# The first two blocks' gate and value products in halves of 128 tokens, taken from whichever job is ready

## The chip, the cores and the metric

The kernel runs on one core of a Trainium2 chip. The core has a matrix engine (TensorE, PE in the profile; its weight loads are the row PEld), a vector engine (VectorE, DVE), a scalar engine (ScalarE, ACT), GpSimd (POOL) and SyncE (SP), which here only issues transfers. Each engine works through its own queue of instructions. The metric is the device time of one execution in microseconds, as the median of several runs.

## The reference

Top-k attention feeds a SwiGLU feed-forward block. Everything is float32.

```python
# attention: batch 8, heads 8, sequence 576, head_dim 64, top_k 32
scores = scale * np.matmul(q, k.transpose(0, 1, 3, 2))
kth = np.partition(scores, -top_k, axis=-1)[..., -top_k:-top_k + 1]
scores = np.where(scores >= kth, scores, -1000000000.0)
scores = scores - np.max(scores, axis=-1, keepdims=True)
attn = np.exp(scores)
attn = attn / (np.sum(attn, axis=-1, keepdims=True) + 1e-09)
x = np.matmul(attn, v)            # then (B,H,S,D) -> (B*S, H*D) = 4608 x 512
# feed-forward: d_model 512, d_ff 1536
g = x @ w_gate
silu = g * (1.0 / (1.0 + np.exp(-g)))
out = (silu * (x @ w_val)) @ w_out
```

## The kernel before

**Units.** Attention is cut into 160 units (batch, query tile, head pair), the head pair running fastest. A batch has four full query tiles of 128 rows and a fifth of 64 rows, in which a unit does half the work (both heads stand side by side). So units 0–15 are full, 16–19 half, 20–35 full again. One turn of the main loop (lines 750 to 810) writes out instructions for several units at different stages. In loop n:

- On even n, PE computes the scores of units n+1 and n+2 (line 306, tile `s`, copied by ACT at line 311 to `sc`), and the products with v of units n-4 and n-3 (line 424, tile `av`), which ACT copies to `xT` (line 440). `xT[kb]` is the transposed input of a feed-forward block of 256 tokens, and `done[kb]` counts what has been written of it.
- ACT weighs unit n-1 (lines 353 and 358: a threshold, then Exp with its sum in `tot`). Its bias comes from a small POOL subtraction (line 341).
- DVE selects the top 32 of unit n by four rounds of MAX8 (line 326) with MATCH_REPLACE8 (line 330) between them. Near the end of the unit comes `normalize` of unit n-1: two DVE instructions on `tot` (lines 369 and 370), and then a multiplication of `e` on POOL (line 376) or ACT (line 374).
- PE transposes the weights of unit n-2 (`turn`, line 390, tile `etps`), and ACT copies them (line 391).

**Rounding of the weights.** The three weight matrices pass through a rounding step in 36 pieces: 24 of gate and value, interleaved by columns, and then 12 of the output matrix. Each piece is a load (line 104, on SP's queue, into one of three `w` buffers), three ACT instructions (112, 114, 115), one on DVE (119) and two on POOL (120, 121). The generator `weights` is advanced by DVE's steps through units 0 to 14, and `ready[0]` tells how many pieces have been written out. A load waits until line 121 has read the buffer that it takes.

**Feed-forward.** There are 18 blocks of 256 tokens. `feed(kb)` is a generator. For each of six steps s it computes the gate product and the value product of two 128-wide slices of d_ff (line 480: 4 contraction chunks, moving operand 256 tokens wide). Every float32 product is two passes in the profile, so counts there are doubled. For the gate, ACT does Tanh, a halving and an addition (505 to 507) and POOL a multiplication (508). For the value it is an ACT copy (512) and a POOL multiplication (513). Block 0 then multiplies by the output matrix directly (line 526, tile `o_ps`); later blocks use seven quarter products instead (line 566, tiles `y_ps` and `x_ps`), with sums and differences on POOL. These need combinations of the output weights, which are built on POOL (lines 169 to 185), most of them only after block 0 no longer needs the plain ones (`plain_done`).

**What sets the order.** No scheduler changes it: every engine executes in the order in which the main loop writes. `pieces(k)` takes up to k feed-forward pieces, as long as `credit` is at least 1. A piece is one slice of gate or value (cost 1), two slices of the output product (cost 1) or half a quarter product (cost 0.75). `share(n)` gives the credit of a loop: a budget, 7.0 before the combined weights exist and 6.4 after, less what PE does for attention in that loop. In a loop `pieces` is called ahead of `turn` for up to two pieces and behind it for the rest. `piece()` (line 670) starts a block only when the whole of its `xT` has been written (`done[kb]` equal to 4 x 256); otherwise it returns 0 and the credit stays unspent. ACT's and POOL's share of a product is put on the lists `on_act` and `on_pool`, and written out at the next flush.

So before the change, block 0 can't begin until query tiles 0 and 1 have been through `av`, in loop 10.

Of the kernel before, what the change touches and what calls it, by code (L numbers as in the profile page):

```python
# [8 lines left out]
AF = mybir.ActivationFunctionType  # L9
ALU = mybir.AluOpType  # L10
FP32 = mybir.dt.float32
# [4 lines left out]
P = 128  # L16
# [4 lines left out]
BLK = 256  # L21
# [4 lines left out]
def kernel(  # L26
# [37 lines left out]
    nc = tc.nc  # L64
# [138 lines left out]
    def need(n):  # L203

        while ready[0] < n:
            next(weight)

    pairs = [(b, hp) for b in range(B) for hp in range(NHP)]
    raw, preps = {}, {}
# [252 lines left out]
    def flush(queue):  # L462
        while queue:
            queue.pop(0)()

    def feed(kb):


# [19 lines left out]
                    on_act.append(lambda: then(ps))  # L488
                yield 1

        plain = kb == 0
        first, late = slice(0, P), slice(P, BLK)

        s32 = x[:].rearrange("p a b -> p (a b)")[:, 0 : MQ * P].rearrange(
            "p (m t) -> p m t", t=P
        )

        for s in range(MS):
            h = ffn.tile([P, 2, BLK], FP32, tag="h", name="h", bufs=MS + 1)
            hs.append(h)  # L500


            def gate(ps, h=h):
                half = ffn.tile([P, 2, BLK], FP32, tag="gv", name="half_g", bufs=3)
                nc.scalar.activation(h[:], ps[:], AF.Tanh, scale=0.5)
                nc.scalar.mul(half[:], ps[:], 0.5)
                nc.scalar.add(h[:], h[:], 1.0)  # L507
                on_pool.append(lambda: nc.gpsimd.tensor_mul(h[:], h[:], half[:]))  # L508

            def value(ps, h=h, s=s):  # L510
                val = ffn.tile([P, 2, BLK], FP32, tag="gv", name="val", bufs=3)
                nc.scalar.copy(val[:], ps[:])  # L512
                on_pool.append(lambda: nc.gpsimd.tensor_mul(h[:], h[:], val[:]))  # L513

            yield from product(wg, s, gate)
            yield from product(wv, s, value)
        o = ffn.tile([P, 2, DM], FP32, tag="o", name="o", bufs=1)
        if plain:
            for t in range(2):
                ps = ps_f.tile([P, DM], FP32, tag="f", name="o_ps")  # L520
                for m in range(MC):
                    need(4 * MS + m + 1)
                    if m == 6:
                        flush(on_act)
                        flush(on_pool)
                    nc.tensor.matmul(  # L526
                        ps[:],
                        hs[m // 2][:, m % 2, t * P : (t + 1) * P],
                        wo[:, m, :],
                        start=(m == 0),  # L530
                        stop=(m == MC - 1),
                    )
                    if m == MC - 1:

                        def finish(ps=ps, t=t):
                            nc.scalar.copy(o[:, t, :], ps[:])
                            store(o[:, t, :], kb * BLK + t * P)

                        on_act.append(finish)
                        if t == 1:  # L540
                            plain_done.append(True)
                    if m % 2 == 1:
                        yield 1
            return
        while len(T[3]) < MQ:
            next(weight)
        DH = DM // 2
# [5 lines left out]

        def quarter(i, ps):
            for m in range(MQ):
                s, r = m // 2, m % 2
                lhsT = {
                    1: lambda: hs[s][:, r, first],
                    2: lambda: hs[s + MS // 2][:, r, first],
                    3: lambda: hs[s][:, r, late],  # L560
                    4: lambda: hs[s + MS // 2][:, r, late],
                    5: lambda: hs[s][:, r, late],
                    6: lambda: s32[:, m],
                    7: lambda: s32[:, m],
                }[i]()
                nc.tensor.matmul(  # L566
                    ps, lhsT, T[i][m], start=m == 0, stop=m == MQ - 1
                )
                if m % 3 == 2:
                    yield 0.75  # L570

        for s in range(MS // 2):
            nc.gpsimd.tensor_tensor(
                s32[:, 2 * s : 2 * s + 2], hs[s][:, :, first], hs[s][:, :, late], ALU.subtract
            )
        yield from quarter(1, y_ps[:, 0])
        flush(on_act)
# [1 line left out]

        for s in range(MS // 2):  # L580
            nc.gpsimd.tensor_tensor(
                hs[s][:, :, late], hs[s][:, :, late], hs[s + MS // 2][:, :, late], ALU.add
            )
        yield from quarter(7, x_ps[:, 1])
        for s in range(MS // 2):
            nc.gpsimd.tensor_tensor(
                s32[:, 2 * s : 2 * s + 2], hs[s][:, :, late], hs[s][:, :, first], ALU.subtract
            )
        yield from quarter(5, x_ps[:, 0])
        a = ffn.tile([P, 2, DH], FP32, tag="gv", name="p57", bufs=3)  # L590
# [21 lines left out]
        flush(on_pool)  # L612
        for s in range(MS // 2):
            nc.gpsimd.tensor_tensor(
                hs[s][:, :, late],
                hs[s + MS // 2][:, :, first],
                s32[:, 2 * s : 2 * s + 2],
                ALU.subtract,
            )
# [44 lines left out]
        on_act.append(rest_x)  # L664

    NU = len(units)
    todo = list(range(NBLK))
    current = []

    def piece():  # L670

# [1 line left out]
            flush(on_act)  # L673
        if len(on_pool) > 1:
            flush(on_pool)
        while True:
            if not current:
                if not todo or done.get(todo[0], 0) < NHP * BLK:
# [182 lines left out]
```

## Time and profile before

| what | us |
|---|---|
| median of 3 runs | 1770.41 (1769.8 to 1771.77) |
| the profiled execution, its own time | 1768.76 |
| its span in the profile | 1767.0 |
| PE busy | 1674.1 (95%) |
| DVE busy | 1483.2 (84%) |
| ACT busy | 1258.6 (71%) |
| POOL busy | 797.3 (45%) |
| chain that ended last, PE's share | 83% |

Busy time is a share of the whole span and hides that the stages differ. In the first 125 us PE is busy for about half of the time and DVE for nearly all of it; from there to the end of attention, near 1700 us, PE is busy for almost all of the time; the last 60 us are the feed-forward work of the last block. The column PEclk in the stretches is the clock granted to PE, as a share of full speed. In the lines of a timeline the first number is the start in us from the start of the span, the second the duration of the group, and the brackets at the end hold the idle time of that engine just before, with what ended it.

### The profile page before, as it was taken

The page shows a single profiled execution, that of the slowest core. Times are in us where ns is not written, and L with a number is a line of the kernel's source. Part 1 is how long each engine was busy: PE and PEld are TensorE (multiplying, and loading weights), DVE is VectorE, ACT ScalarE, POOL GpSimd, SP SyncE. Part 2 cuts the span into 40 slices and gives each one's busy share as a digit, 9 for nine tenths or more (in the row PEclk, how much of TensorE's full clock was granted, in tenths as well). Part 3 has the DMA queues.
Part 4 walks back from the last instruction along what each step waited for, and adds up shares of the span by engine and source line. Part 5 has one row for each costly group of instructions (what it writes and reads, how often), then busy time and mean ns, then how long its engine had stood idle before and what let it go on. Part 6 is the DMA issues. An engine that isn't in the chain of part 4 may idle for free.

```text
span 1767.0 us, 31028 instructions
## 1 busy us (share of the span) xinstructions
PE 1674.1 (95%) x11012; PEld 1386.1 (78%) x11012; DVE 1483.2 (84%) x3371; ACT 1258.6 (71%) x2869; POOL 797.3 (45%) x910
## 2 busy tenths in 40 slices
PE   4559999799999999999999999999999999999999
PEld 3338678687888878888888878888888878888887
DVE  6999898998899899998998988898989889988300
ACT  7789777777767686768777786777776776676531
POOL 4778444334353525353435424444335433535334
PEclk7669999899999999999999999999999999999999
DMA  7443030002100030001200030000300020000000
GB/s 195 130 119 87 27 80 1 13 1 68 30 5 9 14 79 6 13 1 43 54 13 1 13 71 27 1 13 8 90 1 13 1 54 17 13 1 13 1 13 12
DMA packets 109307, 59.68 MB, mean 34 GB/s; under 512 B 88544, under 2 KB 96992, under 8 KB 109152
## 3 DMA queue, kind: packets, MB, share of 16 engines
q1 hardware_dynamic: 108016, 57.37, 12.4%
q8 instruction: 87, 1.43, 0.3%
q14 instruction: 68, 0.56, 0.1%
q10 hardware_dynamic: 1136, 0.33, 0.1%
HBM read 48.23 MB, written 9.44 MB: 33 GB/s over the span
## 4 chain that ended last, share of the span: by engine, by line
PE 83%; DVE 6%; ACT 6%; POOL 3%; issue 1%; SPq 1%; DMA 1%; ACTq 0%; POOLq 0%
PE f L480 40%; PE av L424 9%; PE x_ps L566 9%; PE s L306 7%; PE etps L390 7%; PE y_ps L566 6%; DVE m L326 3%; DVE e L330 2%; PE s L292 2%; ACT e L358 2%; PE kqps L261 1%; PE o_ps L526 1%; ACT e L353 1%; POOL wo L121 1%; ACT et L391 1%
## 5 line engine op out<-in xcount | busy, mean ns | idle before, releaser
L326 DVE MAX8 m<-e 128x8 f32<-128x576 f32 x864 | 615.6, 749 | 3.3
L330 DVE MATCH_REPLACE8 e<-m,e 128x576 f32<-128x576 f32 x576 | 424.1, 743 | 0.0
L480 PE MATMUL f<-xT,wg 128*128 128x256 f32 x1728 | 400.9, 381 | 0.0
L480 PE MATMUL f<-xT,wv 128*128 128x256 f32 x1728 | 399.6, 380 | 0.0
L480 PEld LDWEIGHTS f<-xT,wg 128*128 128x128 f32 x1728 | 323.0, 190 | 50.7 <-issue 8.8
L480 PEld LDWEIGHTS f<-xT,wv 128*128 128x128 f32 x1728 | 323.0, 190 | 49.1 <-issue 7.9
L508 POOL TENSOR_TENSOR h<-h,half_g 128x512 f32<-128x512 f32 x108 | 137.8, 1276 | 353.5 <-ACT h L507 353.3
L358 ACT ACTIVATE e<-e,bias 128x576 f32<-128x576 f32 x288 | 221.1, 775 | 30.5 <-POOL bias L341 27.7
L513 POOL TENSOR_TENSOR h<-h,val 128x512 f32<-128x512 f32 x108 | 137.7, 1275 | 196.0 <-ACT val L512 177.8
L390 PE MATMUL etps<-ident,e 128*128 128x128 f32 (+1 forms) x1312 | 183.4, 282 | 44.1 <-ACT sc L311 20.7
L390 PEld LDWEIGHTS etps<-ident,e 128*128 128x128 f32 (+1 forms) x1312 | 155.3, 143 | 75.4 <-POOL e L376 21.3
L330 DVE MATCH_REPLACE8 e<-m,sc 128x576 f32<-128x576 f32 x288 | 212.0, 743 | 0.0
L353 ACT ACTIVATE e<-sc,m 128x576 f32<-128x576 f32 x288 | 211.1, 785 | 1.3 <-DVE m L326 1.3
L326 DVE MAX8 m<-sc 128x8 f32<-128x576 f32 x288 | 203.4, 743 | 9.1 <-ACT sc L311 9.1
L311 ACT ACTIVATE sc<-s 128x288 f32<-128x288 f32 x512 | 167.1, 413 | 58.8 <-PE s L306 58.5
L306 PE MATMUL s<-kqT 64*128 64x288 f32 x1024 | 175.2, 454 | 34.7 <-ACT et L391 19.3
L391 ACT COPY et<-etps 128x512 f32<-128x512 f32 (+1 forms) x448 | 183.1, 488 | 24.5 <-PE etps L390 24.0
L376 POOL TENSOR_TENSOR e<-e,tot 128x576 f32<-128x576 f32 x140 | 160.2, 1148 | 85.4 <-DVE tot L370 79.1
L369 DVE TENSOR_SCALAR tot<-tot 128x1 f32<-128x1 f32 x288 | 36.0, 145 | 189.6 <-ACT e L358 189.5
L306 PEld LDWEIGHTS s<-kqT 64*128 64x128 f32 x1024 | 96.5, 195 | 82.8 <-issue 25.7
L424 PE MATMUL av<-et,v 128*64 128x128 f32 (+1 forms) x2560 | 161.1, 270 | 0.0
L374 ACT ACTIVATE e<-e,tot 128x576 f32<-128x576 f32 x148 | 118.2, 799 | 39.3 <-DVE tot L370 38.7
(72 smaller groups left out, 2048.8 us busy)
## 6 DMA issues: line engine op xcount, KB each, us to landing
v<-in_v_dram SPq DMA_DIRECT2D x32, 256.0 KB, 3.0
kq_in<-in_k_dram SPq DMA_DIRECT2D x63, 128.0 KB, 2.8
kq_in<-in_q_dram SPq DMA_DIRECT2D x63, 128.0 KB, 3.0
w<-in_moe_w_gate_dram SPq DMA_DIRECT2D x12, 512.0 KB, 3.8
w<-in_moe_w_val_dram SPq DMA_DIRECT2D x12, 512.0 KB, 3.7
w<-in_moe_w_out_dram SPq DMA_DIRECT2D x12, 512.0 KB, 3.6
out_dram<-o SPq DMA_DIRECT2D x38, 128.0 KB, 2.4
out_dram<-o SPq DMA_DIRECT2D x16, 256.0 KB, 2.4
```

Of the source, the lines that this page charges most:

```text
L306: nc.tensor.matmul(ps[:, 0:half], slab[d, q0 : q0 + P], slab[d, k0 : k0 + half])
L311: nc.scalar.mul(sc[:, i * half : (i + 1) * half], ps[:, 0:half], scale)
L326: nc.vector.max(m[:, t, 8 * r : 8 * r + 8], cur[:, hs])
L330: nc.vector.match_replace(e[:, hs], m[:, t, 8 * r : 8 * r + 8], cur[:, hs], LOWEST)
L353: nc.scalar.activation(e[:, hs], sc[:, hs], AF.Prelu, bias=m[:, t, TOP_K - 1 : TOP_K], scale=-1.0, alpha=SMALL,)
L358: nc.scalar.activation(e[:, hs], e[:, hs], AF.Exp, bias=bias[:, t : t + 1], scale=-1.0 / SMALL, accum_out=tot[:, t : t + 1],)
L376: nc.gpsimd.tensor_tensor(e[:, hs], e[:, hs], tot[:, t : t + 1].to_broadcast([P, S]), ALU.mult)
L390: nc.tensor.transpose(ps[0:kl, c * P : (c + 1) * P], e[:, k0 : k0 + kl], ident[:])
L391: nc.scalar.copy(et[0:kl, c0 : c0 + cn, :], ps[0:kl, 0 : cn * P].rearrange("p (c j) -> p c j", c=cn),)
L424: nc.tensor.matmul(av[d, i, 0:ql], weights_, moving, start=c == (0 if last else J), stop=c == (J if last else J - 1),)
L480: nc.tensor.matmul(ps[:, i, :], w[:, kc, m * P : (m + 1) * P], x[:, kc, :], start=(kc == 0), stop=(kc == KC - 1),)
L566: nc.tensor.matmul(ps, lhsT, T[i][m], start=m == 0, stop=m == MQ - 1)
```

## The change

Blocks 0 and 1 get their gate and value products in halves of 128 tokens. `feed_half(kb, t)` takes half t of block kb as soon as that half of `xT` is written. Its matmuls have a moving operand of 128 instead of 256 columns, and one PSUM tile holds four slices instead of two, so a piece is still two slices of one half, with as many columns as before. Block 0's output product becomes `out_half(t)`, one per half. Block 1 goes on with the quarter products in `feed(1)`, which finds its halves in separate tiles (`pair`, `one`).

The six jobs stand in the list `early_jobs`. `piece()` asks them in order, and takes a piece from the first that has one; a job whose input or weights aren't there yields `None`, and the next is asked. While any of the six is left and none is ready, `piece()` returns 0. Only after that do blocks 1 (its quarters) and later run as before. `sure(n)` takes the place of `need(n)` in these jobs: it asks whether a weight piece, and the one after it, have been written out, but doesn't force it. Halves of block 1 beyond the first group also wait until the output product of the same half of block 0 is written out (`told`), since they reuse the seven `h` buffers.

```diff
+    def sure(n):
+        return ready[0] >= min(n + 1, 4 * MS + MC)
...
+    def feed_half(kb, t):
+        while done.get(kb, 0) < NHP * P * (t + 1) or (t and (kb, 0) not in fed):
+            yield None
+        x = xT[kb]
+        cols = slice(t * P, (t + 1) * P)
+        hs = halves_of[kb, t]
+        def product(w, g, then):
+            ps = ps_f.tile([P, 4, P], FP32, tag="f", name="f")
+            for i in range(4):
+                m = 4 * g + i
+                while not sure(4 * (m // 2) + (2 if w is wg else 4)):
+                    yield None
+                for kc in range(KC):
+                    nc.tensor.matmul(ps[:, i, :], w[:, kc, m * P : (m + 1) * P], x[:, kc, cols],
+                                     start=(kc == 0), stop=(kc == KC - 1))
+                if i == 3:
+                    on_act.append(lambda: then(ps))
+                if i % 2 == 1:
+                    yield 1
+        for g in range(MC // 4):
+            while kb == 1 and (t or g) and t not in told:
+                yield None
+            h = ffn.tile([P, 4, P], FP32, tag="h", name="h", bufs=MS + 1)
...
+            yield from product(wg, g, gate)
+            yield from product(wv, g, value)
+        fed.append((kb, t))
...
+    def out_half(t):
+        while (0, t) not in fed or (t and 0 not in told):
+            yield None
...
+        for m in range(MC):
+            while not sure(4 * MS + m + 1):
+                yield None
+            nc.tensor.matmul(ps[:], hs[m // 4][:, m % 4, :], wo[:, m, :],
+                             start=(m == 0), stop=(m == MC - 1))
+            if m == MC - 1:
...
+                told.append(t)
+                if t == 1:
+                    plain_done.append(True)
...
-        for s in range(MS):
+        for s in range(MS if kb > 1 else 0):
...
-    todo = list(range(NBLK))
+    todo = list(range(1, NBLK))
     current = []
+    early_jobs = [
+        feed_half(0, 0), feed_half(0, 1), out_half(0), out_half(1), feed_half(1, 0), feed_half(1, 1),
+    ]
...
     def piece():
...
+        for job in early_jobs[:]:
+            cost = next(job, 0)
+            if cost == 0:
+                early_jobs.remove(job)
+            elif cost is not None:
+                return cost
+        if early_jobs:
+            return 0
```

The gate and value functions inside `feed_half` are those of `feed` on tiles of [128, 4, 128]: the same three ACT instructions and one POOL multiplication, and one ACT copy and one POOL multiplication, each over 512 elements a partition as before. The sums and differences of block 1's quarters are written through `pair(m, t)` and touch the same amounts.

## The prediction

> **What bounds the kernel now.** I read the page's clock row, then engine time by stretch of the opening, then what VectorE (DVE) waits for. A "unit" is one (batch, query tile, head pair); unit n begins where DVE starts its first MAX8 on `sc`. The stretches are units 6–9, 10–13, 14–15, 16–19, 20–27 and 28–29:
>
> ```profile
> core 0: us, PE busy (x) PEld busy (x) DVE busy (x) ACT busy (x) POOL busy (x), PEclk, DMA share, GB/s
> 82.30:128.00 45.70, 24.35 (x154) 17.21 (x152) 45.20 (x103) 38.83 (x85) 35.62 (x33) 0.65 0.41 117
> 128.00:179.80 51.80, 50.04 (x296) 42.13 (x292) 48.69 (x103) 46.86 (x101) 45.45 (x40) 0.98 0.33 99
> 179.80:200.60 20.80, 20.80 (x121) 13.74 (x120) 20.73 (x48) 16.82 (x38) 16.89 (x16) 1.00 0.00 1
> 200.60:230.10 29.50, 28.86 (x199) 18.15 (x198) 22.36 (x50) 21.46 (x53) 5.73 (x8) 1.00 0.25 63
> 230.10:319.20 89.10, 88.66 (x620) 74.44 (x618) 79.91 (x185) 64.70 (x149) 44.15 (x50) 1.00 0.11 28
> 319.20:339.10 19.90, 11.04 (x86) 7.88 (x82) 19.83 (x48) 13.08 (x33) 3.91 (x5) 0.80 0.07 28
> ```
>
> Until 128 us PE is half idle and DVE is full (45.2 of 45.7). From 128 to 319 both are nearly full. In units 28–29 PE is half idle again: the feed-forward work has caught up. So opening PE work can only pay through DVE's idle time up to unit 27. All of it is norm(n-1) waiting for the Exp of the weigh step on ScalarE (ACT):
>
> ```profile
> 149.82 0.15 DVE L369 TENSOR_SCALAR tot<-tot 128x1 f32<-128x1 f32 x1 [2.12 <-ACT e L358]
> ...
> 210.12 0.15 DVE L369 TENSOR_SCALAR tot<-tot 128x1 f32<-128x1 f32 x1 [5.35 <-ACT e L358]
> ...
> 260.10 0.15 DVE L369 TENSOR_SCALAR tot<-tot 128x1 f32<-128x1 f32 x1 [3.20 <-ACT e L358]
> ...
> 284.31 0.15 DVE L369 TENSOR_SCALAR tot<-tot 128x1 f32<-128x1 f32 x1 [3.51 <-ACT e L358]
> ...
> 305.40 0.15 DVE L369 TENSOR_SCALAR tot<-tot 128x1 f32<-128x1 f32 x1 [0.39 <-ACT e L358]
> ```
>
> Each has a twin of 0.60 behind it, so the stalls are 2.7 (unit 11), 6.0 (16), 3.8 (22), 4.1 (24) and 1.0 (26); with 0.3 in unit 13, 17.9 us in all. Those of 16, 22, 24 and 26 are PE's: weigh stands on ACT behind the xT copy, the copy behind av, and av behind PE's backlog. The unit after starts 5.2 to 6.4 us after av ends (av 207.5, 257.6, 281.7, 302.8). That of unit 11 is another kind:
>
> ```profile
> 138.06 1.29 POOL L508 TENSOR_TENSOR h<-h,half_g 128x512 f32<-128x512 f32 x1 [1.95 <-ACT h L507]
> ...
> 145.87 0.69 ACT L112 ACTIVATE size<-w 128x512 f32<-128x512 f32 x1 [2.86 <-DMA w<-in_moe_w_out_dram]
> ```
>
> GpSimd (POOL) meets the first gate product before its input is there and waits; the weight piece queued behind it (L120, L121) comes late; SP issues the next weight load only when L121 frees the buffer; ACT sits in L112 until it lands; weigh is behind L112.
>
> **What the Trainium skill says.** "TensorE: Matmul & The Clock Gate", under "Architectural detail", calls the queues of ACT, DVE and GpSimd strict FIFO, while PE can pull a weight load ahead of running matmuls. The two lines above show the first. For the second:
>
> ```profile
> 144.44 0.76 PE L390 MATMUL etps<-ident,e 128*128 128x128 f32 x5 [0.48 <-POOL e L376]
> 145.04 1.24 PE L480 MATMUL f<-xT,wv 128*128 128x256 f32 x5
> ...
> 144.94 1.17 PEld L480 LDWEIGHTS f<-xT,wv 128*128 128x128 f32 x6
> ```
>
> The load for f starts at 144.94 and its matmul at 145.04, 0.11 later, beside a transpose that takes its 109 ns turn. The same page, "Back-to-back issue gap", gives load-and-matmul streams 81 ns at N=128 against 56 alone (bf16), 1.45 times: my upper estimate. "GPSIMD Engine Reference", "Specifications", says POOL shares its SBUF interfaces with VectorE: L119 takes 0.41 us, but 1.43 at 100.97, beside POOL's weight work.
>
> **What the change moves.** It adds no arithmetic. A piece now is 8 passes of 256 columns; f x16 takes 3.62 us, less 0.38 for one pass's duration, over 15: 216 ns a pass, 1.73 us a piece. A half piece has 16 passes of 128 columns. No row shows that shape as a product. Lower end 109.5 ns (nine transposes, 1.15 less 0.27 over 8), upper 1.45 x 109.5 = 159, and 190 if an f weight load's whole duration (190 ns) were in the open. I take 110, since the trace hid such a load in 110: 1.76 us a piece.
>
> The planner's credits leave every loop's budget nearly alone; what differs is where work exists. Pieces per loop, from the program orders and the credit rule, before/after: loops 6, 7, 9: 0/4, 0/5, 0/3; 10–12: 14/14; 13: 7/3; 14: 3/4; 15–19: 13/13; 20: 4/3; 21, 22: 10/10; 23: 6/5.5; 24: 3/3; 25: 5.25/3; 26: 3/0; 27: 2.25/0. Sums are 70.5 each; from turn 27 on PE's order is identical. Twelve pieces, 20.7 us of PE, go into DVE-bound units, but that isn't the gain.
>
> *Loops 6–9, the price.* PE has room (24.35 of 45.7). ACT and POOL receive three gates and three values: 3 x (1.47 + 0.46) = 5.8 us on ACT, 6 x 1.28 = 7.7 on POOL. Unit 6: sc copies end at 91.4 as now, the gate runs 91.4–92.9, and POOL's gate product stands ahead of the weight piece that now runs 90.40–93.05. That piece ends at 96.85, +3.8. The load which then lands at 96.92 (3.85 after its L121) lands at 100.65; weigh(6), now at 98.60, at 102.35. Norm(6)'s second half, 2.96 later as in unit 11, at 105.35; unit 8 starts 3.04 after it, at 108.4 instead of 105.4: 3.0 lost, unit 11's stall. Behind it round, gate, et and value put weigh(7) at about 114.0 (now 109.4); its norm ends at 116.9, unit 9 starts at 119.95 against 116.0: another 1.0. Loop 8 has no pieces and 1.5–2 us of ACT waits, so weigh(8) is in time. Longer L119s mostly fall ahead of these stalls. **Cost 4.0.** If POOL finds the gate ready: 0.
>
> *Loops 10–16.* Loops 10–12 are unchanged; so is unit 11's stall, I assume. In loop 13 PE loses 4 pieces, but two blocks aren't there to take: PE idles until et(11) frees PSUM banks, about 177.9. s, av and two pieces then finish some 2.5 us earlier; loop 14's extra piece takes 1.76 of it back. The av of loop 16 ends 0.8 sooner. **Gain 0.8**; bounds 0 and 3.
>
> *Loops 16–19.* These units last 5.8 us with ACT at 21.46 of 29.5. Two gates with values (3.9 us) replace output copies, and POOL mixes their products with the weight sums (1.3 each) ahead of the next bias. **Cost 1.0**; bounds 0 and 3.
>
> *Loops 20–27.* PE runs unbroken from 224. One piece fewer by loop 22: av 1.73 earlier, and unit 22's stall shrinks by that. Half a piece fewer in loop 23: 0.87. In loop 25, 2.25 fewer (3.9 us) remove unit 26's stall, 1.0. Sum 3.6. Some 19 half pieces here cost 0.03 each more: −0.6. **Gain 3.0.** The nearly nine pieces gone from 25–27 save no more: DVE's 9.95 us a unit is next.
>
> h slots (`bufs` 7) are covered by the waits on `told`; o_ps is costed at nothing new (same 24 matmuls). SP has fewer instructions between; no load is moved past another. Without PE's idle half as cover, the 12 pieces would cost 20.7.
>
> **Sum.** +4.0 − 0.8 + 1.0 − 3.0 = +1.2. The profiled span 1767.0 becomes 1768.2; with the 1.76 around it (1768.76 in all), 1770.0. The median, 1770.41, stands 1.65 higher: **1771.5**. I call 0.2%, 3.5 us, the least that can be told from no change.
>
> **Rivals.**
> *Faster:* PE is the bound and the moved work is free: POOL isn't held in loops 6–8 (−4.0), nor in 16–19 (−1.0): 1766.5; with the upper bound of loop 13, 1764. For: PE warm there already at 85 us, and POOL idles 10 us in units 6–9. Against: strict order. The 17.9 us of stalls is a wall that it can't reach.
> *Slower:* POOL's wait ahead of the weight pieces repeats. Price 3.0 each; my sum is 2.3 short of the bound, so one repetition, at loop 9 or among the biases of 17–19, decides; two give 1777.5. For: the page shows it at the first gate it ever meets. Against: in units 12–15 it doesn't recur.
> *Slower passes:* at 159 ns a half piece costs 0.8 more; 23 of them in loops 14–22 and about 5 net of 10–12 give +22: 1793. At 120 ns, +4.
> *It doesn't happen:* excluded, the program order has the halves at turn 4.
>
> **Numbers.** No telling difference 0.40; faster 0.33; slower 0.27, of which 0.06 is the passes. Dropping the slow passes and the outer ends leaves 1763 to 1779; the likeliest's own range is 1767 to 1774.
>
> **What would show it.** Unit 8 starting near 108.4 with DVE's L369 waiting about 2 us in unit 7, and ACT's L112 on a w load before it; PE idle near 175; half passes 110 ns apart; stalls of 22 and 24 down to 2.1 and 1.5–3, none in 26; unit 28 within 3 us of 319.2. Wrong if unit 7 has no stall (faster), if stalls appear in units 8–10 or 17–19 beyond 1 us, or if passes stand over 115 ns apart.

## The result, and the profile after

The changed kernel takes 1779.85 us (median of 5 runs, 1775.66 to 1780.54) against 1770.41 (1767.38 to 1773.02) for the kernel before, measured beside it. The ratio is 1.0049, with a 95% interval of 1.0032 to 1.0067: slower by half a per cent. Forecast were 1771.5 us and "no telling difference", with a range up to 1779.

The profiled execution is the shortest of the five (1775.66, span 1773.9, that is 6.9 us over the span before). A second set of runs of the same kernel, the first experiment, has a profile 9.9 us over. The two agree up to unit 28 within 0.5 us.

First the engine time by stretch, cut at the same units as before (6–9, 10–13, 14–15, 16–19, 20–27, 28–29):

```profile
core 0: us, PE busy (x) PEld busy (x) DVE busy (x) ACT busy (x) POOL busy (x), PEclk, DMA share, GB/s
82.80:133.00 50.20, 39.94 (x322) 35.89 (x322) 46.83 (x104) 42.90 (x93) 41.15 (x37) 0.88 0.36 107
133.00:189.60 56.60, 50.14 (x386) 39.07 (x384) 49.15 (x104) 47.61 (x103) 48.13 (x42) 0.97 0.30 91
189.60:209.80 20.20, 20.20 (x112) 12.45 (x109) 20.13 (x49) 14.13 (x32) 10.56 (x11) 1.00 0.04 14
209.80:240.10 30.30, 29.52 (x287) 25.67 (x286) 22.39 (x50) 23.44 (x57) 16.97 (x17) 1.00 0.22 54
240.10:328.50 88.40, 78.89 (x671) 67.96 (x670) 80.07 (x184) 60.74 (x144) 32.96 (x41) 0.97 0.13 34
328.50:348.40 19.90, 13.48 (x77) 9.58 (x75) 19.83 (x47) 12.32 (x31) 2.69 (x4) 0.60 0.01 1
```

PE did get its work early: 39.9 us busy in units 6–9, where it was 24.4. But these units now last 50.2 us instead of 45.7, units 10–13 last 56.6 instead of 51.8, and units 20–27, with PE idle for 9.5 us, are only 0.7 shorter. The gain was to come there. From the start of unit 6 to that of unit 20 the changed kernel takes 9.6 us longer. DVE's waits make up 8.0 of it (18.8 us instead of 10.8), the rest is DVE's busy time. So what was added is mainly waiting, and DVE's waits for the weigh step show where (`normalize` is L373 now; the second wait of each pair, 0.60, is left out):

```profile
105.33 0.15 DVE L373 TENSOR_SCALAR tot<-tot 128x1 f32<-128x1 f32 x1 [2.47 <-ACT e L362]
...
156.84 0.15 DVE L373 TENSOR_SCALAR tot<-tot 128x1 f32<-128x1 f32 x1 [2.55 <-ACT e L362]
...
185.75 0.15 DVE L373 TENSOR_SCALAR tot<-tot 128x1 f32<-128x1 f32 x1 [1.96 <-ACT e L362]
...
219.60 0.15 DVE L373 TENSOR_SCALAR tot<-tot 128x1 f32<-128x1 f32 x1 [5.67 <-ACT e L362]
...
269.84 0.15 DVE L373 TENSOR_SCALAR tot<-tot 128x1 f32<-128x1 f32 x1 [2.46 <-ACT e L362]
...
293.72 0.15 DVE L373 TENSOR_SCALAR tot<-tot 128x1 f32<-128x1 f32 x1 [3.18 <-ACT e L362]
304.84 0.15 DVE L373 TENSOR_SCALAR tot<-tot 128x1 f32<-128x1 f32 x1 [0.37 <-ACT e L362]
```

In order: unit 7 has a new stall; unit 11's has grown from 2.12; unit 13 has a new one; 16's is as it was (5.35 before); 22's and 24's are smaller (3.20, 3.51), yet far from gone; 25 has a new one of 0.97 with its twin. Unit 26's stall is gone.

The new stall of unit 7 is the one that the prediction drew, engine by engine:

```profile
93.22 1.29 POOL L511 TENSOR_TENSOR h<-h,half_g 128x512 f32<-128x512 f32 x1 [2.34 <-ACT h L510]
94.46 1.31 POOL L120 TENSOR_TENSOR size<-size,w 128x512 int32<-128x512 int32 x1
...
101.36 0.69 ACT L112 ACTIVATE size<-w 128x512 f32<-128x512 f32 x1 [3.22 <-DMA w<-in_moe_w_val_dram]
```

POOL waits 2.34 us for the first gate it meets; the weight piece behind it (L120, then L121) runs late; ACT sits 3.22 us in L112 for the weight load that this piece released late; the weigh step that unit 7 needs is behind that. Unit 8 begins at 109.1, forecast at 108.4, at 105.4 before.

The stall of unit 13 was not drawn. POOL, ACT and PE around it:

```profile
171.66 1.29 POOL L516 TENSOR_TENSOR h<-h,val 128x512 f32<-128x512 f32 x1 [3.60 <-ACT val L515]
...
179.11 0.69 ACT L112 ACTIVATE size<-w 128x512 f32<-128x512 f32 x1 [4.76 <-DMA w<-in_moe_w_out_dram]
...
175.61 1.13 PE L540 MATMUL o_ps<-wo,h 128*128 128x512 f32 x2 [1.02 <-POOL wo L121]
179.50 0.65 PE L394 MATMUL etps<-ident,e 128*128 128x128 f32 x4 [2.76 <-POOL e L380]
180.60 1.33 PE L394 MATMUL etps<-ident,e 128*128 128x128 f32 x5 [0.45 <-POOL e L380]
181.72 3.19 PE L540 MATMUL o_ps<-wo,h 128*128 128x512 f32 x4
186.35 1.13 PE L540 MATMUL o_ps<-wo,h 128*128 128x512 f32 x2 [1.44 <-POOL wo L121]
```

At the start of the first half's output product (`out_half(0)`, taken in loop 12) two flushes write the last value product onto POOL's queue, ahead of the weight pieces of loop 12. POOL waits 3.60 us for it. The pieces behind it are late, so the next load and the weigh step behind it are too (ACT, 4.76), and PE, already multiplying by the output matrix, waits for the very pieces of `wo` that POOL is late with (1.02, 1.44), and for `e` in between.

### The profile page after: what moved, and what is told of

The parts are those of the page before. It is cut to its first block, busy times and chain, and to the rows that moved or that the text cites. A ratio compares the mean times of both kernels' runs of the same rounds, so it can differ in the third digit from the quotient of the medians.

```text
span 1773.9 us, 31789 instructions
## 1 busy us (share of the span) xinstructions
PE 1682.4 (95%) x11396; PEld 1402.8 (79%) x11396; DVE 1485.0 (84%) x3371; ACT 1258.9 (71%) x2869; POOL 799.1 (45%) x910
## 3 DMA queue, kind: packets, MB, share of 16 engines
q1 hardware_dynamic: 108016, 57.37, 12.4%
## 4 chain that ended last, share of the span: by engine, by line
PE 80%; ACT 8%; DVE 6%; POOL 3%; issue 2%; SPq 1%; DMA 1%; ACTq 0%; POOLq 0%
PE f L572 37%; PE av L428 9%; PE x_ps L638 9%; PE s L310 7%; PE y_ps L638 6%; PE etps L394 6%; DVE m L330 3%; DVE e L334 2%; PE f L488 2%; ACT e L362 2%; PE s L296 2%; PE kqps L265 1%; ACT e L357 1%; PE o_ps L540 1%; ACT et L395 1%
## 5 line engine op out<-in xcount | busy, mean ns | idle before, releaser
L572 PE MATMUL f<-xT,wg 128*128 128x256 f32 x1536 | 355.5, 381 | 0.0
L572 PE MATMUL f<-xT,wv 128*128 128x256 f32 x1536 | 355.0, 380 | 0.0
L572 PEld LDWEIGHTS f<-xT,wg 128*128 128x128 f32 x1536 | 286.9, 190 | 44.2 <-issue 6.9
L572 PEld LDWEIGHTS f<-xT,wv 128*128 128x128 f32 x1536 | 287.2, 190 | 43.8 <-issue 7.1
L608 POOL TENSOR_TENSOR h<-h,half_g 128x512 f32<-128x512 f32 x96 | 122.4, 1275 | 322.7 <-ACT h L607 322.6
L613 POOL TENSOR_TENSOR h<-h,val 128x512 f32<-128x512 f32 x96 | 122.5, 1276 | 183.8 <-ACT val L612 159.5
L373 DVE TENSOR_SCALAR tot<-tot 128x1 f32<-128x1 f32 x288 | 36.7, 146 | 195.3 <-ACT e L362 195.0
```

The source lines that it names most:

```text
L572: nc.tensor.matmul(ps[:, i, :], w[:, kc, m * P : (m + 1) * P], x[:, kc, :], start=(kc == 0), stop=(kc == KC - 1),)
```

## The experiments

All kernels are the changed one with the edit named, except `before_later`, which is the kernel before with an edit. The table gathers the runs; stretches are in us between the starts of the units named, from one profile each.

| version | median us | ratio to before, 95% interval | 6–9 | 9–13 | 13–17 | 17–20 | 20–28 |
|---|---|---|---|---|---|---|---|
| before | 1770.41 | 1 | 33.7 | 50.2 | 46.4 | 17.4 | 89.1 |
| after | 1779.85 | 1.0049 (1.0032–1.0067) | 38.2 | 51.9 | 49.2 | 18.0 | 88.4 |
| again | 1778.71 | 1.0053 (1.0041–1.0066) | 38.2 | 52.2 | 49.4 | 18.0 | 88.4 |
| late_start | 1771.29 | 1.0007 (1.0001–1.0014) | 33.8 | 49.9 | 46.9 | 17.4 | 90.5 |
| block0 | 1773.62 | 1.0023 (1.0014–1.0032) | 37.5 | 51.9 | 48.4 | 17.4 | 86.9 |
| pool_later | 1774.47 | 1.0029 (1.0018–1.0040) | 35.7 | 51.8 | 49.2 | 18.0 | 88.4 |
| before_later | 1767.61 | 0.9987 (0.9980–0.9993) | 33.2 | 49.0 | 46.7 | 17.4 | 89.1 |
| late_later | 1771.30 | 1.0001 (0.9993–1.0009) | 33.4 | 50.2 | 46.7 | 17.4 | 90.5 |
| out_flush | 1779.33 | 1.0054 (1.0041–1.0066) | 37.1 | 53.1 | 48.8 | 18.0 | 88.4 |
| wo_margin | 1782.56 | 1.0065 (1.0051–1.0078) | 38.2 | 52.0 | 48.9 | 19.9 | 89.1 |
| wo_margin_later | 1778.44 | 1.0041 (1.0028–1.0054) | 35.0 | 50.8 | 48.7 | 19.9 | 90.5 |
| hold12 | 1783.20 | 1.0078 (1.0064–1.0091) | 38.2 | 52.2 | 52.7 | 18.0 | 88.5 |
| both | 1773.27 | 1.0020 (1.0012–1.0028) | 35.0 | 50.8 | 47.5 | 18.0 | 88.5 |
| three | 1773.67 | 1.0020 (1.0012–1.0027) | 35.5 | 50.9 | 44.9 | 19.9 | 89.1 |

Single executions of one kernel differ by 3 to 7 us between lowest and highest. Of the changed kernel there are two profiles; of the 3.1 us by which they differ, 2.6 lie behind unit 28. So the stretches tell more than a single span does.

### again: the changed kernel unchanged

> The changed kernel, nothing altered. Its profiled execution (1775.66) was the fastest of five, the others stood near 1780, with a lower mean PE clock (0.97 against 0.986). If the loss is a fixed set of waits, the ratio to before is again 1.003 to 1.007 and unit 7 lasts about 15.6 us, unit 13 about 16.6. If PE's clock in the first 125 us decides, a profile with a mean clock near 0.97 shows units 6 to 9 some 4 us longer than the first profile did.

1778.71 us, 1.0053. The loss is real, and its profile has every stretch of the table within 0.3 us of the first one's. The clock of PE in the opening isn't the cause: with a mean clock of 0.974 units 6–9 take the same 38.2 us as in the first profile with 0.986.

### late_start: halves, but not before loop 10

```diff
+        if loop[0] < 10:
+            return 0
         for job in early_jobs[:]:
```

> The half jobs aren't asked before loop 10, so the pieces per loop are those of the kernel before (4, 7, 3, 7, 3, 7 in loops 10 to 15), but of 128 columns for two blocks. Theory 1 (queue): the loss is POOL's wait for a gate or value ahead of weight pieces; unit 7 is back at 12.0 us and unit 8 at 10.6, unit 11 keeps its 15, unit 13 depends on the early flush of the output product; time 1 to 4 us over the kernel before. Theory 2 (load): early ACT and POOL work costs wherever it stands; then this is as fast as the kernel before, within 2 us. Theory 3 (passes): 384 half products with two passes each at 112 ns against 192 at 216 ns cost 3 us more PE time wherever PE is the bound; time at least 3 us over before in units 14 to 27.

The halves are all there, and so are the tiles and the order of jobs; only the twelve pieces of loops 6, 7 and 9 come later, and each loop takes as many pieces as before the change. The time is 1771.29, and units 6 to 20 take what they took before (unit 20 at 230.6 instead of 230.1). So nearly the whole loss comes from starting early. Whether it is the place in POOL's queue or the early work as such, this run can't tell: both theories allow the measured time; `pool_later` separates them. The third theory wanted 3 us for the passes. What is left in this profile up to unit 28 lies in units 20–27, 1.4 us:

```profile
230.60:321.10 90.50, 90.05 (x807) 81.30 (x805) 79.98 (x185) 64.82 (x149) 44.19 (x50) 1.00 0.11 27
```

PE is busy for 90.05 of 90.50 us there, and was for 88.66 of 89.10. The trace has 23 half pieces there, where the kernel before has as many whole ones. Their price is thus 0.06 us each.

### block0: only block 0 in halves

```diff
-            if kb == 1:
+            if kb == 0:
                 return halves_of[1, t][m // 4][:, m % 4 : m % 4 + 2, :]
...
-        for s in range(MS if kb > 1 else 0):
+        for s in range(MS if kb > 0 else 0):
...
-        feed_half(0, 0), feed_half(0, 1), out_half(0), out_half(1), feed_half(1, 0), feed_half(1, 1),
+        feed_half(0, 0), feed_half(0, 1), out_half(0), out_half(1),
```

> Only block 0 in halves and early; block 1 is fed as before, whole, when both its halves are there. The pieces in loops 6 to 13 are those of the changed kernel, loop 15 has 3 instead of 7, loops 16 and 17 none. If the loss lies in the early start of block 0, units 7 to 13 and so about 9 us of loss at unit 14 stay; unit 16's stall of 6.3 us shrinks to 1 or less since PE has 5 pieces fewer there, but the stalls of units 22 to 26 grow to the kernel before's 8.9. The time is then 0 to 4 us under the changed kernel. If block 1's halves are what costs, it is within 1 us of the kernel before.

Block 1 is computed whole again. The loss up to unit 14 is the same (189.4 against 189.6), so it belongs to block 0's early start. Units 20–27 take 86.9 us, 2.1 fewer than before the change, though they hold more pieces than the changed kernel's (31.5 against 24.5): with wide passes and block 0 out of the way, the gain that the prediction hoped for is there in part. By the medians 1773.62 us recovers 5 to 6 of the 9 us; by the profiles it is 3.2 to 3.7 us ahead at unit 28. It is more than the 0 to 4 us expected, but unit 16's stall did not shrink to 1 us (DVE is idle for 5.5 us in that unit, 6.6 in the changed kernel).

### pool_later: POOL's multiplications one loop later

```diff
-        flush(on_pool)
+        if not 6 <= n < 14:
+            flush(on_pool)
```

This is the flush behind the transposes. Without it a waiting product goes onto POOL's queue when two are waiting or when the next loop begins, and thus behind the weight pieces of its loop.

> The changed kernel, but in loops 6 to 13 POOL's gate and value multiplications are written out at the start of the next loop instead of just behind the transposes, so the weight pieces and the normalization of that loop stand ahead of them; the amount of work is the same. Theory 1 (queue): unit 7 falls from 15.6 to 12 to 13 us, unit 11 from 15.7 to 12 to 14, unit 13 keeps its stall of 3; the time falls by 4 to 8 us. Theory 2 (load): same ACT and POOL work, so unit 7 stays above 14.5 and the time falls by less than 2 us.

1774.47 us. POOL's and ACT's lines for unit 7, and DVE's wait:

```profile
90.56 1.30 POOL L120 TENSOR_TENSOR size<-size,w 128x512 int32<-128x512 int32 x1
...
95.55 1.29 POOL L511 TENSOR_TENSOR h<-h,half_g 128x512 f32<-128x512 f32 x1
...
98.09 0.73 ACT L112 ACTIVATE size<-w 128x512 f32<-128x512 f32 x1
...
102.09 0.15 DVE L373 TENSOR_SCALAR tot<-tot 128x1 f32<-128x1 f32 x1 [0.49 <-ACT e L362]
```

The weight piece now runs at 90.56, where it ran at 94.46; the gate's product runs at 95.55 without a wait; ACT finds its weights landed; DVE's wait falls from 2.47 to 0.49. Unit 7 lasts 12.3 us instead of 15.6, and unit 11 12.3 instead of 15.7. So the cause of these two stalls is shown. Part of it is given back: units 8, 10 and 12 become 0.5, 1.0 and 2.3 longer. Over units 7 to 12 together 3.0 us are gained, of which 1.3 are waits of DVE and 1.7 its busy time, from 71.7 to 70.0 us. The head start over the changed kernel, 3.2 us at unit 8, is 2.9 at unit 17. The stretch 13–17 stays at 49.2: what costs time there is something else.

### before_later: the same edit in the kernel before

```diff
-        flush(on_pool)
+        if not 10 <= n < 14:
+            flush(on_pool)
```

> The kernel before, with POOL's gate and value multiplications of loops 10 to 13 written out one loop later (no halves). Its unit 11 has the same stall of 2.7 us as unit 7 of the changed kernel. Queue theory: unit 11 falls from 15.0 to 12 to 13 us. If PE's backlog then binds, the gain is given back as a longer stall in unit 16, and the time is within 1.5 us of before; if DVE's chain binds up to unit 16, the time falls by 2 to 3 us.

```profile
138.53 2.26 POOL L376 TENSOR_TENSOR e<-e,tot 128x576 f32<-128x576 f32 x2
140.74 0.20 POOL L341 TENSOR_TENSOR bias<-m 128x2 f32<-128x2 f32 x1
140.89 1.30 POOL L508 TENSOR_TENSOR h<-h,half_g 128x512 f32<-128x512 f32 x1
143.29 1.29 POOL L513 TENSOR_TENSOR h<-h,val 128x512 f32<-128x512 f32 x1 [1.10 <-ACT val L512]
...
147.01 0.15 DVE L369 TENSOR_SCALAR tot<-tot 128x1 f32<-128x1 f32 x1 [0.48 <-ACT e L358]
```

The gate product's wait of 1.95 us is gone, and DVE's falls from 2.12 to 0.48: unit 11 lasts 12.3 us, not 15.0. Units 12 and 14 give back 1.4 and 1.6, and unit 13 gains 1.3. At 1767.61 us, 0.9987 (0.9980 to 0.9993), this version beats both kernels. The stall of unit 11 was in the profile of before from the start; most of it goes with the place of one multiplication in POOL's queue. But what is gained in the end isn't waiting. Units 10–14, in the kernel before and in this one:

```profile
127.99:190.66 62.67, 60.91 (x384) 50.82 (x381) 59.52 (x127) 57.73 (x127) 55.97 (x49) 0.99 0.27 82
127.82:189.56 61.74, 60.30 (x382) 50.66 (x379) 56.71 (x127) 57.66 (x127) 55.66 (x49) 0.98 0.28 83
```

DVE's busy time (the third of the engines) falls by 2.8 us, as its step of the weight pieces, L119, now takes 7.1 us in sum instead of 10.5; its idle time grows from 3.1 to 5.0, for unit 11's falls from 2.7 to 1.1 and units 12, 13 and 14 have 1.7, 1.1 and 1.0. That leaves 0.9 us; the rest of the gain in the time, 1.2 to 3.5 us by the interval, isn't found in this stretch.

### late_later: late_start with POOL's multiplications later

```diff
+        if loop[0] < 10:
+            return 0
...
-        flush(on_pool)
+        if not 10 <= n < 14:
+            flush(on_pool)
```

> The changed kernel with two edits: the early jobs are not asked before loop 10, and POOL's gate and value products of loops 10 to 13 come one loop later. It joins the version that gave the whole loss back with the edit that made the kernel before faster. If the two are independent, the time is 1771.3 - 2.8 = 1768.5, ahead of the kernel before by about 2 us and level with or 1 us behind the kernel before with that edit (1767.6); unit 11 lasts 12.3 us instead of 14.6. If halves of 128 tokens are of use once POOL's wait is gone, it is under 1767. If 2 us or more of it are given back in units 12 to 16, it is 1770 or more.

1771.30 us, where 1768.5 was expected if the two edits were independent: no gain over late_start. Unit 11 lasts 12.3 us as expected, but 9–13 is no shorter than before (50.2): unit 10 takes 11.4 instead of 10.6, with a wait of 0.6, and unit 12 takes 14.6 instead of 12.6. Units 20–27 again take 90.5. The two edits don't add up, and halves bring nothing even where POOL's wait is gone. Why unit 10 waits here and not in `before_later` was not pursued.

### out_flush and wo_margin: the two waits around unit 13, one at a time

`out_flush` takes away the flushes that put the last value product ahead of loop 12's weight pieces; `wo_margin` lets an output piece be taken only when two more weight pieces have been written out, so that PE shouldn't run into them.

```diff
-        flush(on_act)
-        flush(on_pool)
+        if t == 1:
+            flush(on_act)
+            flush(on_pool)
```

```diff
-        while not sure(4 * MS + 2):
+        while not sure(4 * MS + 2 + 2):
...
-            while not sure(4 * MS + m + 1):
+            while not sure(4 * MS + m + 1 + 2):
```

> The changed kernel without the two flushes at the start of the first half's output product, so the last value multiplication of the second half isn't put into POOL's queue ahead of loop 12's weight pieces before ACT has its copy. Theory 1 (queue): unit 13's stall of 2.95 goes to below 1, units 7 to 11 are as in the changed kernel, the time falls by 2 to 3.5 us. Theory 2 (load): unit 13's stall comes from late weight loads in general and stays above 2; no difference.

> The changed kernel, but block 0's output product asks for output-weight pieces with two more pieces written out behind them, so PE doesn't stand in loop 13 in front of a weight piece that POOL has yet to write. Loop 13 has 2 pieces instead of 3, loop 25 has 3.75 instead of 3, the others are the same. Queue theory for PE: loop 14's scores and av stood behind those waits (1.0 and 1.4 us in the profile of the changed kernel); from unit 13 to unit 17 it falls from 49.2 us to 46 to 47.5, and the time by 1.5 to 3 us. Rival: from unit 14 to 17 PE is bound by its 12 pieces and the idle time in loop 13 comes from the missing work, so the stretch stays above 48.5 and the time within 1 us.

> wo_margin and pool_later together. If POOL's queue (units 7 and 11, 3 us at unit 17 by pool_later) and PE's wait for output weights (1.5 to 3) are separate, the sum is 4.5 to 6 us under the changed kernel, near 1773. If the second is only another face of the first, it is as fast as pool_later alone, within 1 us of it.

`out_flush` shortens unit 13 as it should (16.6 to 13.6 us), and loses nearly all of it by unit 17, 2.2 us in unit 16 alone (12.4 to 14.6): unit 17 begins at 222.7, as in the repeat of the changed kernel (222.6). The 2 to 3.5 us expected in the time are not there. PE in loops 13 and 14:

```profile
181.63 1.12 PE L541 MATMUL o_ps<-wo,h 128*128 128x512 f32 x2 [1.60 <-POOL wo L121]
184.31 2.08 PE L541 MATMUL o_ps<-wo,h 128*128 128x512 f32 x2 [1.56 <-POOL wo L121]
186.32 2.29 PE L310 MATMUL s<-kqT 64*128 64x288 f32 x8
```

PE still waits twice for `wo`, and then runs at half clock: two output matmuls take 2.08 us instead of 1.12, eight of `s` 2.29 instead of 1.24 (the last section has the clock).

`wo_margin` moves a piece out of loop 13 and gains nothing there either (48.9), while unit 18 gets a stall of 2.25 us. Its median is higher, 1782.56, though its interval overlaps that of the changed kernel; its profile is 2.3 us later at unit 28. With POOL's multiplications later as well (`wo_margin_later`), 1778.44, where 1773 was expected: worse than `pool_later` alone, by the same stall of unit 18 and 2 us in units 20–27.

### hold12: fill loop 13 with three pieces of loop 12

The prediction's reading of loop 13, that PE idles there for want of pieces, was a second theory: 12 pieces moved to loops 6–9 are missing in loop 13, while loops 14 and 15 stay full.

```diff
+        if loop[0] == 12:
+            return 0
         for job in early_jobs[:]:
```

> The changed kernel with one edit: in loop 12 no feed-forward piece is taken, so three pieces move from loop 12 to loop 13 (12: 0 instead of 3, 13: 6 instead of 3); the budgets of all other loops give the same as in the changed kernel. Nothing of the opening (units 6 to 11) is touched. Theory that loop 13 runs out of work (units 13 to 16 grew because PE stands idle in loop 13 for want of gate and value pieces, while 14 and 15 are as full as before): PE's idle time around 176 to 181 us goes, the stretch from unit 13 to unit 17 shrinks from 49.2 us to at most 47.5, and unless unit 12 gets longer the time falls by 1.5 to 3 us, to about 1776. Rival (what holds units 13 to 16 back is where POOL waits for block 0's last value and where the output weights arrive, not how much PE has to do): the stretch stays at 48.5 us or more, the time within 1.5 us of the changed kernel's.

Slower: 1783.20 us, and the stretch 13–17 grows to 52.7. The theory's forecast failed. POOL, ACT and PE:

```profile
182.33 1.28 POOL L516 TENSOR_TENSOR h<-h,val 128x512 f32<-128x512 f32 x1 [6.45 <-ACT val L515]
...
189.74 0.67 ACT L112 ACTIVATE size<-w 128x512 f32<-128x512 f32 x1 [6.36 <-DMA w<-in_moe_w_out_dram]
...
186.26 2.08 PE L540 MATMUL o_ps<-wo,h 128*128 128x512 f32 x2 [3.12 <-POOL wo L121]
```

The last value product now comes a loop later, POOL's wait for it grows from 3.60 to 6.45 us, and all that followed from it follows again, later and longer. From unit 13's start to the products with v of loop 14, PE's idle time falls only from 5.7 to 3.6 us while three pieces, 5.4 us, are added. The idle time was not filled by more pieces in the same loop: it comes behind them, at the point where PE needs the output weights. The stated rival is closer, but it too had the time wrong (within 1.5 us of the changed kernel's), and `av` of loop 14 comes 3.6 us later. How much of that is the added work and how much the later waits isn't separated: the edit moves both, and PE runs at half clock for 6.83 us here (185.52 to 192.35), for 3.41 in the changed kernel.

### three and both: the waits taken away together

`three` joins the edits of `pool_later`, `out_flush` and `wo_margin`; `both` only the first two.

> The changed kernel with three edits at once, each tried before: POOL's gate and value products of loops 6 to 13 one loop later; no flush at the start of the first half's output product; output pieces two weight pieces later. Theory that two waits in turn (POOL's for the last value in unit 13, then PE's for output weights being rounded in loop 14) hold PE's restart, so that taking one away alone shows nothing: the stretch from unit 13 to unit 17 falls to 46 to 47.5 us, and the time is 2 us or more under that of the first edit alone (1774.5), near 1772. Rival (the lack of work in loop 13 is what counts, and no wait): the stretch stays at 48 us or more, and the time is 1773 to 1778.

> The changed kernel with two of the last three edits: POOL's gate and value products of loops 6 to 13 one loop later, and no flush at the start of the first half's output product; the output pieces are not put off. Theory that the two waits of units 13 and 14 (POOL's for the last value, PE's for output weights being rounded) must both go: the stretch from unit 13 to unit 17, 49.2 us in the changed kernel and 44.9 with all three edits, stays at 47.5 or more, and the time is within 1.5 us of the first edit alone (1774.5). Rival (POOL's wait alone was to blame, and the delay only brought the stall of 2.3 us in unit 18): the stretch is 46.5 or less, unit 18 has no stall beyond 0.5, and the time is 1772 or less, under all three edits together (1773.7).

With all three the stretch 13–17 falls to 44.9 us, 1.5 less than before the change and 4.3 less than after. DVE doesn't wait at all from unit 13 to unit 15. One output piece, some 1.7 us of PE, has left the stretch. With two edits it is 47.5. Singly, `pool_later`, `out_flush` and `wo_margin` had 49.2, 48.8 and 48.9. So the waits stand one behind the other, and taking one away uncovers the next. The time follows only in part: 1773.67 and 1773.27, the same, and 0.8 and 1.2 us under `pool_later` alone, where 2 us or more were expected of `three`. `three` loses in unit 18 what it gains in unit 16, a stall of 2.26 us: at unit 19 the two stand at 228.4 and 228.6. The output pieces put off must be done somewhere, and units 17 and 18 last 5.8 us with nothing to hide them. Both remain 0.2% slower than the kernel before, by intervals that exclude no change: 2.1 to 2.5 us are lost by unit 9 and some 2 more by unit 20, and units 20–27 give back 0.5 at most.

One number ties these runs together. The table gives, from unit 13's start, when the products with v (`av`) of loops 14 and 16 start on PE:

| | av of loop 14 | av of loop 16 | unit 17 |
|---|---|---|---|
| before | 15.0 | 38.9 | 46.4 |
| late_start | 15.3 | 39.4 | 46.9 |
| after | 15.7 | 41.7 | 49.2 |
| block0 | 15.7 | 40.9 | 48.4 |
| out_flush | 14.6 | 41.3 | 48.8 |
| both | 14.1 | 40.0 | 47.5 |
| three | 9.4 | 37.4 | 44.9 |
| hold12 | 19.3 | 45.2 | 52.7 |

In all fourteen profiles, of the versions left out of this table too, unit 17 begins 7.5 us after that `av` of loop 16. DVE's stall in unit 13 doesn't set it; PE does: in the changed kernel it works through units 14 and 15 without a gap (20.20 of 20.20 us). What DVE saves before that, it waits for in unit 16 (8.8 us idle in `out_flush`, 6.6 in the changed kernel).

## Why the prediction was wrong, step by step

The sum was +4.0 − 0.8 + 1.0 − 3.0 = +1.2. Measured, from the first profile of the changed kernel and from its repeat (the sums are those of unrounded values):

| step | predicted | after | again |
|---|---|---|---|
| up to unit 6 | 0 | +0.4 | +0.4 |
| loops 6–9 (to unit 9) | +4.0 | +4.5 | +4.5 |
| loops 10–12 (9–13) | 0 | +1.7 | +2.0 |
| loops 13–16 (13–17) | −0.8 | +2.8 | +3.0 |
| loops 16–19 (17–20) | +1.0 | +0.6 | +0.6 |
| loops 20–27 | −3.0 | −0.7 | −0.7 |
| from unit 28 on | 0 | −2.5 | +0.1 |
| sum | +1.2 | +6.9 | +9.9 |

*Loops 6–9: right, mechanism and size.* POOL's wait, the late load, ACT in L112, weigh behind it; `pool_later` shows it by taking it away. That is unit 7, 3.6 us longer, 3.1 of it waiting. For unit 8 another 1.0 was forecast, from a late weigh(7), and 1.2 came. No stall shows there, because L119 took 1.0 us longer and filled the time; the Exp of that weigh ended at 117.92, just before DVE's second instruction on `tot` at 117.95. Either alone would have cost about 1 us, an estimate from these times. The faster rival, in which POOL isn't held and the moved work is free, is excluded. The Trainium skill's "TensorE: Matmul & The Clock Gate" ("Architectural detail") says that ACT's, DVE's and GpSimd's queues are strict FIFO; the waits of 2.34, 3.60 and 6.45 us with ready weight work behind them agree.

*Loops 10–12: "unchanged" was wrong.* I counted pieces per loop, which are the same. But the last product of loop 9 leaves its gate and value to be written out at the start of loop 10, ahead of the weigh step:

```profile
133.82 0.57 ACT L508 ACTIVATE h<-f 128x512 f32<-128x512 f32 x1
...
135.29 0.57 ACT L515 COPY val<-f 128x512 f32<-128x512 f32 x1
135.76 1.32 ACT L315 ACTIVATE sc<-s 128x288 f32<-128x288 f32 x4
```

That is 2 us of ACT in front of loop 10's score copies, and two multiplications on POOL. Unit 10 lasts 12.0 us instead of 10.6 (0.60 of waiting, 0.6 for one slower L119), unit 11 0.7 more. `late_start` has unit 10 back at 10.6, but it takes away the pieces of loops 6 and 7 too; that it is loop 9's leftover is read from the order, not shown by a run of its own. A loop's neighbours inherit its unflushed work.

*Loops 13–16: the step that failed, 3.6 us.* The count of pieces was right (3 instead of 7 in loop 13, 4 instead of 3 in 14), PE does idle near 175, and the extra piece of loop 14 does cost what was said (`av` of loop 16 follows that of 14 by 26.0 us, before 23.9). What failed is "s, av and two pieces then finish some 2.5 us earlier": they came 0.7 us later. I took PE's idle time as slack to be won. It was a wait for POOL and for weights still being rounded, since the early start brings the output product to where its weights are only just made. `three`, with the edits against these waits joined, has the `av` of loop 14 at 9.4 instead of 15.7. The waits also cost PE its clock: half for 3.41 us in this stretch, where the kernel before has full clock from 160 to 216 us. The term 2.5 − 1.76 measured −0.7 − 2.1. The slower rival had this mechanism, POOL's wait ahead of weight pieces, but named loop 9 and the biases of 17–19 as places, and said against itself that units 12–15 show no such wait. The profile of before showed none: the kernel before begins its output product at 191.0 us, 2.6 us after its last weight piece is rounded; the changed one begins it at 167.65, 29.9 us before its last piece is, and its flushes come with it.

*Loops 16–19: right in size, not in cause.* 0.6 where 1.0 stood, all of it in unit 18. The prediction had ACT full and POOL late with a bias. What ACT waits for is PE:

```profile
230.52 0.37 ACT L444 COPY xT<-av 128x256 f32<-128x256 f32 x1 [1.02 <-PE av L428]
```

The `av` of loop 18 starts 5.9 us after unit 17 begins, 5.4 before the change. Why PE is later there was not pursued.

*Loops 20–27: direction right, size wrong by 2.3.* Unit 26's stall of 1.0 went as said. Those of 22 and 24 shrank by 0.7 and 0.3 instead of 1.7 and 0.9, and unit 25 has a new one of 1.0, from POOL:

```profile
299.32 1.26 POOL L625 TENSOR_TENSOR p<-p,p 128x512 f32<-128x512 f32 x1
300.56 2.09 POOL L686 TENSOR_TENSOR h<-h,xT 128x256 f32<-128x256 f32 x3
302.62 1.14 POOL L380 TENSOR_TENSOR e<-e,tot 128x576 f32<-128x576 f32 x1
303.72 0.19 POOL L345 TENSOR_TENSOR bias<-m 128x2 f32<-128x2 f32 x1
```

The sums of block 1's quarters stand ahead of the bias there, and ACT waits 4.19 us for it. With block 1 early, this work comes two loops earlier than before. `late_start` and `block0` have no such stall. The term "−0.6" for slower passes, 19 half pieces at 0.03, had the price at half: `late_start` and `late_later` pay 1.4 for 23 of them (90.5 against 89.1). In the changed kernel the trace has 14 in these units, by the same price some 0.9 us (an estimate).

*Passes: right in kind, and the rival of 159 ns excluded.* A group of the new passes:

```profile
91.60 3.74 PE L488 MATMUL f<-xT,wv 128*128 128x128 f32 x32
```

Less one pass's 0.27, over 31, that is 112 ns a pass, against 110 forecast; a half piece takes 1.79 us instead of 1.73. "Back-to-back issue gap" of the same page led to the upper estimate of 159 ns, by the ratio of its two bf16 figures; this ratio isn't seen. The extra load per 128 columns is hidden almost wholly. Still, 0.06 us times 23 pieces is the 1.4 of `late_start`.

*Chances.* Slower had 0.27, most of it for a mechanism that turned out to be the one at work. The range missed its upper end by 0.9 us. Bounds of 0 and 3 on loops 13–16, both gains, left out a loss, and that is what happened.

## What to carry to other kernels

Moving matrix work into idle time moves its followers on the in-order queues, too: for every piece, ask in which order its flushes stand to the work of another chain (here the weight pieces), and what waits behind an input that isn't there yet. Idle time of an engine is only slack if what ends it isn't late itself; an early start that reaches a consumer of something still being produced (here the output weights) has to wait for the producer, which isn't early. And when a page shows a stall in the old kernel whose cause is one instruction's place in a queue, move that instruction first: that alone gave 0.13% here (0.07 to 0.20), where the larger change lost 0.5%. Then look where the wait went: here it came back in the next three units, and what stayed as gain was a shorter busy time of DVE.

## What the runs showed of the hardware

Short waits can cost PE its clock. The Trainium skill, "TensorE: Matmul & The Clock Gate", Part 1, says that PE falls to half its clock after an idle window of about 3.4 us. The length agrees: the granted clock, 1.0 or 0.5 in these traces, changes only in steps of 3.41 us, the end of a trace aside. But the window need not be idle throughout. In `out_flush` PE was at work for 1.13 of 3.41 us, between two waits, and the next two windows were at half clock:

```profile
180.02:183.43 3.41, 1.13 (x3) 0.30 (x2) 3.10 (x5) 3.41 (x6) 3.25 (x4) 1.00 0.24 48
183.43:186.84 3.41, 2.53 (x4) 1.01 (x6) 2.46 (x8) 3.41 (x10) 3.33 (x3) 0.50 0.27 108
```

The fourteen profiles, cut into such windows, have 131 falls from full to half clock. Each follows a window with at least 1.34 us of PE idle; and no window at full clock with more than 2.02 us idle was without a fall (ends of matmuls are modelled, so these bounds are rough). In the changed kernel PE was busy for 0.69 us of the window from 177.23, with most of the wait of 2.76 us in it; in the next, at half clock, four output matmuls took 3.19 us, where the first four took 1.88 at 167.65. A wait of PE that leads to such a window is longer in its effect than in its bracket.

The DVE step of a weight piece (L119) takes 0.41 us alone, and up to 1.50 beside POOL's work (at 161.07 in the kernel before, beside an L120), though not beside all of it: at 147.30 it took 0.40 wholly beside an L121. Through it a shift of POOL's work by a few us makes a unit 0.6 to 1.0 us longer or shorter without any wait in the profile; in `before_later` that is where the gain of units 10–14 lies.
